# Moving a routing step behind two reductions in an attention + top-k mixture-of-experts kernel, and pinning its weight copies to slots

## The chip, the cores and the metric

The kernel runs on one core of one Trainium2 chip, in one launch. The metric is the device time of that launch in microseconds (us). A core has five engines with queues of their own, each of which works strictly in its order: PE (TensorE, matrix products and transposes), DVE (VectorE), ACT (ScalarE), POOL (GpSimd) and SP (SyncE, which here only issues transfers). Transfers run on 16 DMA engines, whoever issued them.

## The reference

Attention with normalised queries and keys over 8 batches, 12 heads, 448 positions, 64 dimensions, and then a gated mixture of 8 experts over the 3584 resulting rows of width 768:

```python
q_n, k_n = rmsnorm(q, g_q), rmsnorm(k, g_k)        # x / sqrt(mean(x*x) + 1e-6) * g
scores = matmul(q_n, k_n.T) / sqrt(64)
attn = softmax(scores)
x = matmul(attn, v).transpose(0, 2, 1, 3).reshape(N, 768)
logits = x @ w_gate                                 # 768 x 8
expert_idx = argmax(logits); gate_w = softmax(logits)[expert_idx]
for e in range(8):                                  # the 80 rows of largest gate_w of each expert
    out[tok] = gate_w[tok] * (relu(x[tok] @ w1[e]) @ w2[e])      # w1 768x1024, w2 1024x768
```

Rows that no expert keeps are zero in the output.

## The kernel before, in words

**Tiling.** A *group* `g` is four heads of one batch, so there are 24 groups (`NG`), three (`NQ`) to a batch `b`. A group has 7 *blocks* (`RD`) of 64 keys. For each of the 168 blocks, `score` (L351) lets PE multiply 64 keys by all 448 queries for the four heads into the PSUM tile `ps` (PSUM is the small memory that PE writes), and ACT takes the exponential into `at` (L362). `av` (L365) multiplies by the values `vt` into `po`, and `presum` (L387) adds the `at` tiles up on DVE into `sm`, the denominators-to-be, at L392 and L394.

**Preparing a group.** For q (`a` = 0) and k (`a` = 1): ACT squares the loaded tile `qk` into `sq` (`square`, L270). DVE reduces it to the sums of squares `ms` (`squares`, L278). `rstd` (L286) lets ACT take a logarithm and an exponential of `ms` into `rs` (L289, L290) and DVE refine `rs` with three small instructions (L291 to L293). `normalise` (L300) lets DVE multiply `qk` by `rs` into `qn` (L306). `transp` (L328) transposes `qn` on PE into a PSUM tile `tp`, which ACT copies out as `qkT` (L349 for k, L347 for q).

**Routing a batch.** After a batch's third group, `zl` (L396) lets PE compute 48 products to unnormalised logits and denominators. `gate1` and `gate1t` copy, add and transpose them. `gate1v` (L439) takes the reciprocals `rz` (L445, the *quotients*), multiplies (`lx`, L453) and sends `rz` off by SP (L460). `gate2` (L465) sums to the logits `lg` (L468) and finds the maximum and the equality mask `eq`. `gate2x` (L480) is ACT's exponential `lex` and the copy `eqb`. `gate2b` (L486) sums and inverts to the gate weight `gw`. `gate2i` and `gate2p` are POOL's share: it packs `gw` and row numbers into `info` (L504 to L521). `merge` (L524) then keeps a running list of the best 80 rows of each expert; its steps `row` (transposes `gw` on PE, copied by ACT at L543), `experts`, `own`, `counts`, `place`, `turn` are mixes of small PE, ACT and DVE work.

**What sets the order.** It is written out by hand. There are 84 *slots* (`NS`), each with two score blocks and the two `av` of the slot before. Four tables say what else a slot emits: `begins`, `pre` (behind the scores), `mid` (behind `presum`) and `end`, with `ahead` in front of `end`. Each engine receives its part in that order. `b0` is the slot in which a batch's last group starts (in the second table loop) or in which a group starts (in the first). With 10.5 slots to a batch, odd and even batches meet the groups' preparation differently.

**PSUM tiles.** `ps`, the k-side `tp`, `zl` and the scratch tiles of `merge` take turns in two buffers named `sc`. PE can't begin a `ps` before ACT has emptied the tile two turns back.

**The weights.** Experts 0 to 2 are loaded once into SBUF, converted to bf16 on the way (`fetch_held`, L669; POOL issues, behind a small DVE memset of the tile). The others are converted into a scratch in DRAM (`stage_w`, L201, two halves for each matrix, POOL issues, nothing in front of it) and fetched later by SP (`fetch_late`). The output is first filled with zeros by SP.

**The tail.** After the last slot come the last batch's routing and the eight experts in turn (L966 on).

Of the kernel before, what the change touches and what calls it, by code (L numbers as in the profile page):

```python
# [11 lines left out]
BF16 = mybir.dt.bfloat16  # L12
# [9 lines left out]
def kernel(  # L22
# [13 lines left out]
    nc = tc.nc  # L36
# [3 lines left out]
    E = moe_w_gate.shape[1]  # L40
# [13 lines left out]
    NQ = H // 4  # L54
# [9 lines left out]
    NW0 = 3  # L64
    wb_dram = nc.dram_tensor("wb_scratch", (E - NW0, 2, DM * F), BF16, kind="Internal").ap()

    cpool = ctx.enter_context(tc.tile_pool(name="const", bufs=1))
# [130 lines left out]
    def staged(e, i):  # L198
        return wb_dram[e - NW0, i].rearrange("(c p f) -> p c f", p=128, c=(DC, FC)[i])

    def stage_w(e, i, half):  # L201
        src = (moe_w1, moe_w2)[i][e].rearrange("(c p) f -> p c f", p=128)
        c = src.shape[1] // 2
        nc.gpsimd.dma_start(out=staged(e, i)[:, half * c:half * c + c],
                            in_=src[:, half * c:half * c + c])
# [27 lines left out]
    with av_stack:  # L233
# [117 lines left out]
        def score(r):  # L351
            g, x = divmod(r, RD)
            T0, T1 = st[g]["T0"], st[g]["T1"]
            ps = scps.tile([128, 2, 512], F32, tag="sc", name="ps")
            at = apool.tile([128, 2, S], F32, tag="at", name="at")
            for u in range(2):
                for hh in range(2):
                    d = slice(hh * D, (hh + 1) * D)
                    nc.tensor.matmul(ps[u * 64:u * 64 + 64, hh, :S],  # L359
                                     T1[d, u, x * 64:(x + 1) * 64], T0[d, u, :],  # L360
                                     start=True, stop=True)
            nc.scalar.activation(at[:], ps[:, :, :S], AF.Exp)  # L362
            st[g]["at%d" % x] = at

        def av(r):  # L365
            g, x = divmod(r, RD)
            vt, at = st[g]["v"], st[g]["at%d" % x]
            if x == 0:
                po = pops.tile([128, 2, 512], F32, tag="po", name="po")
                other = po if g < NG - 1 else tpps.tile([128, 2, 512], F32, tag="tp", name="po")  # L370
                st[g]["po"] = (po, other)
            po = st[g]["po"]
            for u in range(2):
                p = slice(u * 64, u * 64 + 64)
                for hh in range(2):
                    nc.tensor.matmul(po[u][hh * D:(hh + 1) * D, u, :S],  # L376
                                     vt[p, hh * NX + x, :], at[p, hh, :],
                                     start=(x == 0), stop=(x == RD - 1))
            if x == RD - 1:
                st[g]["us"] = upool.tile([128, 2, S], F32, tag="us", name="us")  # L380

                n = 2 if g < NG - 1 else 1
                nc.scalar.copy(st[g]["us"][:, :n], po[0][:, :n, :S])  # L383
                if n < 2:
                    nc.vector.tensor_copy(st[g]["us"][:, n:], po[1][:, n:, :S])

        def presum(r):  # L387
            g, x = divmod(r, RD)
            s = st[g]
            if x == 1:  # L390
                s["sm"] = smpool.tile([128, 2, S], F32, tag="psm", name="sm")
                nc.vector.tensor_add(s["sm"][:], s["at0"][:], s["at1"][:])  # L392
            elif x > 1:
                nc.vector.tensor_add(s["sm"][:], s["sm"][:], s["at%d" % x][:])  # L394
# [298 lines left out]
        begins, pre, mid, end = {}, {}, {}, {}  # L693

        def at_slot(where, s, f, *a):
            where.setdefault(s, []).append((f, a))

        ahead = {}

        def first(s, f, *a):  # L700
            ahead.setdefault(s, []).append((f, a))
# [15 lines left out]
        for g in range(NG):  # L717
            b0 = g * RD // 2
            at_slot(begins, max(b0 - 11, -10), load_qk, g)
            at_slot(begins, b0 - 4, load_v, g)  # L720
            if g:
                for a in range(2):
                    at_slot(mid, b0 - 7 + a if g > 1 else -1, square, g, a)
                    at_slot(end, b0 - 7 + a if g > 1 else -1, squares, g, a)
                at_slot(mid, b0 - 5 if g > 1 else 0, rstd, g)
                for a in range(2):
                    at_slot(mid, b0 - 5 + a if g > 1 else 0, normalise, g, a)
            if g:
                for a in (0, 1) if g == 1 else (1, 0):
                    at_slot(end, b0 - 2 + (a if g == 1 else 0), transp, g, a)  # L730
            if g < NG - 2:
                i = g % NQ
                x0 = ((NQ * (g // NQ) - 1) * RD // 2 + 10 + 3 * i) if g >= NQ else 6 + 3 * i
                at_slot(end, b0 + 6 if i == NQ - 1 else x0, xout, g)
        for b in range(B):
            b0 = (NQ * b + NQ - 1) * RD // 2
            if b == B - 1:
                at_slot(end, b0 + 3, zl, b, range(NQ - 1))
                at_slot(end, b0 + 4, xout, NG - 2)
                at_slot(end, b0 + 4, zl, b, range(NQ - 1, NQ))  # L740
                at_slot(end, b0 + 4, gate1, b)
                at_slot(end, b0 + 4, xout, NG - 1)
                at_slot(end, b0 + 5, gate1t, b)
                at_slot(mid, b0 + 6, gate1v, b)
                continue
            first(b0 + 5, zl, b, range(NQ))
            first(b0 + 5, gate1, b)
            at_slot(end, b0 + 6, gate1t, b)
            at_slot(mid, b0 + 7, gate1v, b)
            at_slot(mid, b0 + 7, gate2, b)  # L750
            at_slot(mid, b0 + 8, gate2i, b)
            at_slot(end, b0 + 8, gate2x, b)
            at_slot(pre, b0 + 9, gate2b, b)
            at_slot(pre, b0 + 9, gate2p, b)
            for t, fs in enumerate(merge(b)):


                if b == B - 2 and t > 3:
                    at_slot(end, b0 + 12 + t, fs[0])
                    continue  # L760
                s = 15 + b % 2 if b < B - 2 else 13
                (first if t else lambda *a: at_slot(end, *a))(
                    b0 + (10, 10, 12, s, 18 + b % 2, 20 + b % 2)[t], fs[0])
                for n, f in enumerate(fs[1:]):
                    at_slot(end, b0 + (10, 11, 12, s)[t], f)
        at_slot(begins, 0, load_wgs)
        at_slot(end, NS - 6, weights_early)
        at_slot(end, NS, weights_late)
# [7 lines left out]
                in_=zeros[:, :].unsqueeze(1).to_broadcast([128, DM // ZW, ZW])))  # L776
        for e in range(E):
            for i in range(2):
                s = 9 + 23 * (2 * e + i) // 5
                if e < NW0:  # L780
                    at_slot(mid, s, fetch_held, e, i)
                    continue
                for half in range(2):
                    at_slot(begins, s + 2 * half, stage_w, e, i, half)


        wps = scps.tile([128, 2, 512], F32, tag="sc", name="wps")
# [3 lines left out]
        for s in range(-10, NS + 6):  # L791
            for f, a in begins.pop(s, []):
                f(*a)
            S2 = [r for r in (2 * s, 2 * s + 1) if 0 <= r < NG * RD]
            A2 = [r for r in (2 * s - 2, 2 * s - 1) if 0 <= r < NG * RD]

            for r in A2:
                if r % RD == RD - 1 and r < A2[-1]:
                    av(r)
            for r in S2:  # L800
                score(r)
            for f, a in pre.pop(s, []):
                f(*a)
            for r in A2:
                presum(r)
            for f, a in mid.pop(s, []):
                f(*a)
            for r in A2:
                if r % RD < RD - 1 or r == A2[-1]:
                    av(r)  # L810
            for f, a in ahead.pop(s, []) + end.pop(s, []):
                f(*a)
        assert not ahead
        assert not begins and not pre and not mid and not end
    mpool = ctx.enter_context(tc.tile_pool(name="moe_sb", bufs=2))

# [11 lines left out]
    b = B - 1  # L828
# [27 lines left out]
    ahead = tpool.tile([128, NT, CAP], BF16, tag="ahead", name="ahead")  # L856
# [187 lines left out]
```

## Time and profile before

| | |
|---|---|
| time, median of 3 runs | 424.39 us (422.96 to 424.91) |
| the profiled execution | 423.0 us, its span 421.3 us |
| PE busy | 399.1 us, 95% |
| DVE busy | 357.5 us, 85% |
| ACT busy | 314.9 us, 75% |
| POOL busy | 73.5 us, 17% |
| granted PE clock | 0.998 of full speed |
| HBM read, written | 101.11 MB, 39.89 MB |

The span runs from the first instruction to the last; around it lie 1.7 us. Slots fill it from 15.6 us to about 356 us, the tail the rest. "Busy" counts an engine's instructions without its waits; an instruction of 128x896 elements takes about 1 us on DVE or ACT, and PE does a slot's 16 score rows in 1.5 us. In a row of the timeline, the bracket at the end is the time for which the engine stood idle before it, and what ended that.

### The profile page before, as it was taken

The numbers are of one execution on the slowest core, as the hardware profiler recorded it, in microseconds if no ns is written. First come the engines' busy times: TensorE is split into PE (matmuls) and PEld (weight loads), VectorE is DVE, ScalarE is ACT, GpSimd is POOL, SyncE is SP. The second block draws the span as 40 slices with busy tenths as digits, with TensorE's granted clock in tenths as the row PEclk, the third lists the DMA queues.
The fourth block names the chain that finished last, engine by engine and source line by source line (L and its number), as shares of the span: only waits on it lengthen the run. The fifth ranks groups of instructions, "written<-read, shape, count | busy, mean of one in ns | idle before, by whom it ended". The sixth has DMA issues, their size and how long they took to land.

```text
span 421.3 us, 12543 instructions
## 1 busy us (share of the span) xinstructions
PE 399.1 (95%) x5289; PEld 194.9 (46%) x5289; DVE 357.5 (85%) x641; ACT 314.9 (75%) x479; POOL 73.5 (17%) x118
## 2 busy tenths in 40 slices
PE   6799999999989999999899999999999999889993
PEld 6334444444444445444444444443444443448882
DVE  5699889998999999989999999989999779735550
ACT  5898979997889799979798799878997784202120
POOL 2000001301040205100420024001500050134321
PEclk9999999999999999999999999999999999999999
DMA  7355599999959999999799969999799298869981
GB/s 261 123 149 140 152 224 317 282 254 268 287 166 206 326 230 274 242 237 320 234 236 233 338 172 195 232 286 338 170 237 312 59 358 211 270 213 339 342 301 47
DMA packets 75983, 100.91 MB, mean 240 GB/s; under 512 B 8344, under 2 KB 65176, under 8 KB 75928
## 3 DMA queue, kind: packets, MB, share of 16 engines
q1 hardware_dynamic: 59856, 70.53, 52.2%
q0 software_dynamic: 15776, 29.13, 36.1%
q8 instruction: 41, 0.67, 0.6%
q10 hardware_dynamic: 296, 0.46, 0.4%
q14 instruction: 14, 0.11, 0.1%
HBM read 101.11 MB, written 39.89 MB: 335 GB/s over the span
## 4 chain that ended last, share of the span: by engine, by line
PE 69%; DMA 12%; DVE 10%; ACT 5%; issue 2%; SPq 0%; POOLq 0%; DVEq 0%; ACTq 0%
PE ps L359 26%; PE po L376 26%; DMA w_sb<-wb_scratch 5%; PE zl L411 4%; DMA qk<-in_k_dram 4%; PE tp L314 3%; PE xp L314 3%; DVE ms L278 2%; DVE sm L394 2%; DMA xr_scratch<-xb 2%; PE py L992 1%; DVE qn L306 1%; PE ph L973 1%; ACT qkT L349 1%; DMA xg<-xr_scratch,idxG 1%
## 5 line engine op out<-in xcount | busy, mean ns | idle before, releaser
L359 PE MATMUL ps<-qkT 64*64 64x448 f32 x1344 | 147.9, 548 | 7.6 <-ACT qkT L349 3.2
L362 ACT ACTIVATE at<-ps 128x896 f32<-128x896 f32 x168 | 146.4, 931 | 2.5 <-PE ps L359 1.6
L376 PE MATMUL po<-at,vt 64*64 64x448 f32 x1344 | 142.4, 537 | 0.1
L394 DVE TENSOR_TENSOR sm<-sm,at 128x896 f32<-128x896 f32 x120 | 132.0, 1100 | 2.9
L376 PEld LDWEIGHTS po<-at,vt 64*64 64x64 f32 x1344 | 50.0, 133 | 74.9 <-issue 64.3
L359 PEld LDWEIGHTS ps<-qkT 64*64 64x64 f32 x1344 | 43.1, 132 | 73.2 <-issue 23.5
L278 DVE TENSOR_REDUCE ms<-sq 128x14 f32<-128x896 f32 (+1 forms) x50 | 51.9, 1044 | 6.6 <-ACT sq L270 6.4
L306 DVE TENSOR_TENSOR qn<-qk,rs 128x896 f32<-128x896 f32 (+1 forms) x50 | 52.5, 1052 | 1.9
L270 ACT ACTIVATE sq<-qk 128x896 f32<-128x896 f32 (+1 forms) x50 | 46.3, 929 | 2.8 <-DMA qk<-in_q_dram 2.8
L518 POOL CAST pt<-gw 128x4 bf16<-128x4 f32 x8 | 6.9, 866 | 201.9 <-DVE gw L491 201.9
L977 ACT ACTIVATE h_sb<-ph 128x320 bf16<-128x320 f32 x16 | 7.0, 437 | 39.8 <-PE ph L973 39.8
L654 ACT COPY xb<-xp 128x1024 f32<-128x1024 f32 x24 | 24.3, 1011 | 9.7 <-PE xp L314 9.6
L314 PEld LDWEIGHTS tp<-ident,qn 64*128 64x128 f32 x672 | 23.4, 139 | 11.1 <-issue 5.3
L314 PE MATMUL tp<-ident,qn 64*128 64x64 f32 x672 | 26.9, 226 | 0.0
L383 ACT COPY us<-po 128x896 f32<-128x896 f32 (+1 forms) x24 | 21.4, 893 | 6.2 <-PE po L376 6.2
L392 DVE TENSOR_TENSOR sm<-at 128x896 f32<-128x896 f32 x24 | 25.9, 1081 | 0.0
L347 ACT ACTIVATE qkT<-tp,gqk 128x896 f32<-128x896 f32 x23 | 23.5, 1023 | 0.0
L349 ACT COPY qkT<-tp 128x896 f32<-128x896 f32 x24 | 21.9, 913 | 1.3 <-PE tp L314 1.2
L992 PE MATMUL py<-w_sb,h_sb 128*80 128x384 bf16 (+1 forms) x136 | 22.2, 317 | 0.6 <-DMA w_sb<-wb_scratch 0.6
L996 DVE TENSOR_SCALAR yo<-py,gwT 80x384 f32<-80x384 f32 (+1 forms) x16 | 9.5, 600 | 14.9 <-PE py L992 14.7
L411 PE MATMUL zl<-us,wgs 64*32 64x448 f32 x192 | 21.0, 540 | 0.0
L411 PE MATMUL zl<-sm,zsel 64*32 64x448 f32 x192 | 20.5, 540 | 0.0
(170 smaller groups left out, 412.0 us busy)
## 6 DMA issues: line engine op xcount, KB each, us to landing
wb_scratch<-in_moe_w_dram POOLq DMA_DIRECT2D x20, 768.0 KB, 14.9
w_sb<-wb_scratch SPq DMA_DIRECT2D x9, 1536.0 KB, 8.1
vt<-in_v_dram SPq DMA_DIRECT2D x24, 448.0 KB, 6.3
out_dram<-zeros SPq DMA_DIRECT2D x28, 384.0 KB, 8.2
qk<-in_q_dram SPq DMA_DIRECT2D x23, 448.0 KB, 5.0
qk<-in_k_dram SPq DMA_DIRECT2D x23, 448.0 KB, 6.6
xr_scratch<-xb SPq DMA_DIRECT2D x48, 192.0 KB, 10.2
w_sb<-in_moe_w_dram POOLq DMA_DIRECT2D x6, 1536.0 KB, 15.7
```

Of the source, the lines that this page charges most:

```text
L270: nc.scalar.activation(st[g]["sq%d" % a][:, lo:hi], st[g]["qk"][a][:, lo:hi], AF.Square)
L278: nc.vector.reduce_sum(out=st[g]["ms"][:, a, lo:hi], in_=st[g]["sq%d" % a][:, lo:hi], axis=AX.X)
L306: nc.vector.tensor_mul(qn[:].rearrange("p (x hh) d -> p hh x d", hh=2)[:, h0:h1], qk[:, lo:hi].rearrange("p (hh x) d -> p hh x d", x=NX), ...
L314: nc.tensor.transpose(o, w, one[p, p], tile_position=(p.start, 0))
L349: nc.scalar.copy(T[:], tp[:, :, :S])
L359: nc.tensor.matmul(ps[u * 64:u * 64 + 64, hh, :S], T1[d, u, x * 64:(x + 1) * 64], T0[d, u, :], start=True, stop=True)
L362: nc.scalar.activation(at[:], ps[:, :, :S], AF.Exp)
L376: nc.tensor.matmul(po[u][hh * D:(hh + 1) * D, u, :S], vt[p, hh * NX + x, :], at[p, hh, :], start=(x == 0), stop=(x == RD - 1))
L392: nc.vector.tensor_add(s["sm"][:], s["at0"][:], s["at1"][:])
L394: nc.vector.tensor_add(s["sm"][:], s["sm"][:], s["at%d" % x][:])
L411: nc.tensor.matmul(t[32 * c:32 * c + 32, r, :S], w, x, start=(i == 0), stop=(i == NQ - 1))
L992: nc.tensor.matmul(py[:, :c1 - c0], h_sb[:, fc, :], chunk(e, 1, fc)[:, c0:c1], start=(fc == 0), stop=(fc == FC - 1))
```

## The change

- `gate1v` moves from the middle of slot `b0 + 7` to its end, behind the sums of squares that stand there; `gate2` and `gate2i` move to the end of slot `b0 + 8`, `gate2x`, `gate2b` and `gate2p` to the end of slot `b0 + 9`.
- The q-side normalisation of a group that starts a batch (from the third batch on) goes to a new table `after`, emitted last in its slot, so that `gw` stands in front of it.
- The product `tied` of `merge` goes one slot later.
- The weights: `fetch_held` takes other slots, and each half of `stage_w` gets a slot of its own in `mid`, held there by a one-element DVE memset of `mark` and a POOL copy of that element in front of the DMA.

```diff
+    mark = cpool.tile([1, 4 * (E - NW0)], BF16, name="mark")
+
     def stage_w(e, i, half):
+        n = 4 * (e - NW0) + 2 * i + half
+        nc.vector.memset(mark[:, n:n + 1], 0.0)
+        nc.gpsimd.tensor_copy(mark[:, n:n + 1], mark[:, n:n + 1])
...
-        ahead = {}
+        ahead, after = {}, {}
...
                 for a in range(2):
-                    at_slot(mid, b0 - 5 + a if g > 1 else 0, normalise, g, a)
+                    s = b0 - 5 + a if g > 1 else 0
+                    at_slot(after if not a and g % NQ == 0 and g > NQ else mid, s, normalise, g, a)
...
-            at_slot(mid, b0 + 7, gate1v, b)
-            at_slot(mid, b0 + 7, gate2, b)
-            at_slot(mid, b0 + 8, gate2i, b)
-            at_slot(end, b0 + 8, gate2x, b)
-            at_slot(pre, b0 + 9, gate2b, b)
-            at_slot(pre, b0 + 9, gate2p, b)
+            at_slot(end, b0 + 7, gate1v, b)
+            at_slot(end, b0 + 8, gate2, b)
+            at_slot(end, b0 + 8, gate2i, b)
+            at_slot(end, b0 + 9, gate2x, b)
+            at_slot(end, b0 + 9, gate2b, b)
+            at_slot(end, b0 + 9, gate2p, b)
...
                 for n, f in enumerate(fs[1:]):
-                    at_slot(end, b0 + (10, 11, 12, s)[t], f)
+                    at_slot(end, b0 + (10, 11 + n, 12, s)[t], f)
...
-                s = 9 + 23 * (2 * e + i) // 5
+                n = 2 * e + i
                 if e < NW0:
-                    at_slot(mid, s, fetch_held, e, i)
+                    at_slot(mid, 4 + 9 * n // 2, fetch_held, e, i)
                     continue
                 for half in range(2):
-                    at_slot(begins, s + 2 * half, stage_w, e, i, half)
+                    at_slot(mid, 4 + 9 * (2 * n + half) // 4, stage_w, e, i, half)
...
-            for f, a in ahead.pop(s, []) + end.pop(s, []):
+            for f, a in ahead.pop(s, []) + end.pop(s, []) + after.pop(s, []):
                 f(*a)
```

PE's and SP's queues keep their order. DVE's queue at batch 1, from the end of slot 24 on, before (`rz` to `eq` are the routing's quotients and logits, `ms` the sums of squares of q and k):

```order
L445 RECIPROCAL rz<-zs 128x12x2 x2
L453 TENSOR_TENSOR lx<-zs,rz 128x12x8 x4
L468 TENSOR_REDUCE lg<-lx 128x32
L471 TENSOR_REDUCE lmax<-lg 128x4
L474 TENSOR_TENSOR lex<-lg,lmax 128x32
L476 TENSOR_TENSOR eq<-lg,lmax 128x32
L477 MEMSET eq 64x8
L278 TENSOR_REDUCE ms<-sq 128x14
L394 TENSOR_TENSOR sm<-sm,at 128x896
L278 TENSOR_REDUCE ms<-sq 128x14
L489 TENSOR_REDUCE lsum<-lex 128x4
L491 RECIPROCAL gw<-lsum 128x4
```

and in the changed kernel (lines shift by 5):

```order
L283 TENSOR_REDUCE ms<-sq 128x14
L450 RECIPROCAL rz<-zs 128x12x2 x2
L458 TENSOR_TENSOR lx<-zs,rz 128x12x8 x4
L399 TENSOR_TENSOR sm<-sm,at 128x896
L283 TENSOR_REDUCE ms<-sq 128x14
L473 TENSOR_REDUCE lg<-lx 128x32
L476 TENSOR_REDUCE lmax<-lg 128x4
L479 TENSOR_TENSOR lex<-lg,lmax 128x32
L481 TENSOR_TENSOR eq<-lg,lmax 128x32
L482 MEMSET eq 64x8
```

Both sums of squares now stand in front of the logits; `lsum` and `gw` follow eight rows later, behind two `sm` additions and the three small `nw`, `rs` instructions.

ACT's queue at the same place, before (`lex` and `eqb` are the routing's, `rs` belongs to the normalisation, `qkT` are the copies of the transposed k and q):

```order
L481 ACTIVATE lex<-lex 128x32
L483 CAST eqb<-eq 128x288
L362 ACTIVATE at<-ps 128x896 x2
L289 ACTIVATE rs<-ms,eps 128x28
L290 ACTIVATE rs<-rs 128x28
L349 COPY qkT<-tp 128x896
L347 ACTIVATE qkT<-tp,gqk 128x896
```

and in the changed kernel:

```order
L367 ACTIVATE at<-ps 128x896 x2
L294 ACTIVATE rs<-ms,eps 128x28
L295 ACTIVATE rs<-rs 128x28
L354 COPY qkT<-tp 128x896
L352 ACTIVATE qkT<-tp,gqk 128x896
L486 ACTIVATE lex<-lex 128x32
L488 CAST eqb<-eq 128x288
```

The routing's two instructions moved from in front of the exponentials to behind the copies.

## Rows read from the trace of the kernel before

**Rows 1.** Busy time by engine in stretches from one zl to the next.
```profile
core 0: us, PE busy (x) PEld busy (x) DVE busy (x) ACT busy (x) POOL busy (x), PEclk, DMA share, GB/s
98.10:144.50 46.40, 44.61 (x600) 19.73 (x599) 43.72 (x76) 39.25 (x59) 6.61 (x10) 1.00 0.95 245
144.50:185.54 41.04, 40.93 (x570) 18.40 (x568) 39.67 (x69) 37.12 (x57) 10.32 (x16) 1.00 1.09 253
...
272.97:319.40 46.43, 44.99 (x604) 19.65 (x603) 43.60 (x72) 39.49 (x60) 7.30 (x11) 1.00 1.03 257
```
**Rows 2.** Waits of PE: us in total, times, longest us.
```profile
PE ps L359 <- ACT qkT L349: 3.2, 3, 1.2
...
PE ps L359 <- ACT row L543: 1.3, 3, 0.4
```
**Rows 3.** Timeline of PE, slots 26 to 28: start, us, instructions, idle before.
```profile
116.00 1.08 PE L314 MATMUL tp<-ident,qn 64*128 64x64 f32 x28
117.02 0.98 PE L359 MATMUL ps<-qkT 64*64 64x448 f32 x8
119.24 0.98 PE L359 MATMUL ps<-qkT 64*64 64x448 f32 x8 [1.24 <-ACT qkT L349]
...
121.76 0.33 PE L314 MATMUL mp<-identb,eqb 64*72 64x64 bf16 x8
...
124.20 0.98 PE L359 MATMUL ps<-qkT 64*64 64x448 f32 x8 [0.44 <-ACT row L543]
```
**Rows 4.** Timeline of ACT, the same slots.
```profile
114.47 0.23 ACT L481 ACTIVATE lex<-lex 128x32 f32<-128x32 f32 x1 [0.96 <-DVE lex L474]
...
115.04 1.72 ACT L362 ACTIVATE at<-ps 128x896 f32<-128x896 f32 x2
117.81 0.32 ACT L289 ACTIVATE rs<-ms,eps 128x28 f32<-128x28 f32 x1 [1.06 <-DVE ms L278]
...
118.30 0.89 ACT L349 COPY qkT<-tp 128x896 f32<-128x896 f32 x1
...
119.98 1.72 ACT L362 ACTIVATE at<-ps 128x896 f32<-128x896 f32 x2
```
**Rows 5.** Timeline of DVE, slots 22 to 28.
```profile
101.70 0.63 DVE L424 TENSOR_TENSOR zsb<-zsb,zo 128x448 f32<-128x448 f32 x1 [1.54 <-ACT zo L423]
...
112.00 0.46 DVE L445 RECIPROCAL rz<-zs 128x24 f32<-128x24 f32 x2
...
113.14 0.85 DVE L468 TENSOR_REDUCE lg<-lx 128x32 f32<-128x384 f32 x1
...
114.70 1.09 DVE L278 TENSOR_REDUCE ms<-sq 128x14 f32<-128x896 f32 x1
...
116.70 1.08 DVE L278 TENSOR_REDUCE ms<-sq 128x14 f32<-128x896 f32 x1
117.69 0.18 DVE L489 TENSOR_REDUCE lsum<-lex 128x4 f32<-128x32 f32 x1
...
120.85 1.09 DVE L306 TENSOR_TENSOR qn<-qk,rs 128x896 f32<-128x896 f32 x1
121.86 2.47 DVE L394 TENSOR_TENSOR sm<-sm,at 128x896 f32<-128x896 f32 x2
...
125.29 0.06 DVE L671 MEMSET w_sb<- 128x1 uint32 x1
```
**Rows 6.** The page's group of the sm additions: busy, mean ns, idle before.
```profile
L394 DVE TENSOR_TENSOR sm<-sm,at 128x896 f32<-128x896 f32 x120 | 132.0, 1100 | 2.9
```
**Rows 7.** Timeline of POOL, two rows behind the routing of batches 1 and 4.
```profile
120.92 1.34 POOL L512 TENSOR_TENSOR info<-eq,pt 128x160 bf16<-128x160 f32 x1
...
253.75 3.03 POOL L204 DMA_DIRECT2D wb_scratch<-in_moe_w_dram  x4
```
**Rows 8.** Timeline of SP: the issue of one load of q.
```profile
266.85 0.42 SPq L242 DMA_DIRECT2D qk<-in_q_dram  x1
```
**Rows 9.** Timeline of ACT: the square that needs that load.
```profile
284.67 0.96 ACT L270 ACTIVATE sq<-qk 128x896 f32<-128x896 f32 x1 [0.98 <-DMA qk<-in_q_dram]
```

More of the change, by code (lines that the diff above doesn't have):

```diff
@@ L810 @@
                     av(r)
-            for f, a in ahead.pop(s, []) + end.pop(s, []):
+            for f, a in ahead.pop(s, []) + end.pop(s, []) + after.pop(s, []):
                 f(*a)
-        assert not ahead
+        assert not ahead and not after
         assert not begins and not pre and not mid and not end
```

## The prediction

> **What bounds the kernel now.** I first read the page's busy shares: PE works 95% of the span at full clock, so the kernel can gain only where PE stands still or where it does less, and the change takes nothing from PE. To find where PE stands still I cut the slots into stretches from one batch's `zl` to the next [rows 1]. An even batch's stretch is full: 40.93 us busy of 41.04. An odd batch's stretch has 1.79 us without PE (46.40 less 44.61), and the one that ends at 319.40 is just as long. Batches 1, 3 and 5 make three such stretches. The list of waits then names the cause [rows 2]: three waits of a score for ACT's copy of the transposed k, 3.2 us together, and three for ACT's copy of `row`, 1.3 us together. There is nothing else of size inside the slots. So the question is what holds ACT at these two points.
>
> PE's timeline shows the place [rows 3]: the first score tile of slot 27 starts at 117.02, the second should follow about 0.80 later and starts at 119.24, so 1.42 us are lost; the second tile of slot 28 comes at 124.20, and about 0.6 is lost there (its gap is 0.44 beside a modelled end). ACT's timeline gives the reason [rows 4]: the copy L349 that frees the `sc` buffer starts at 118.30, because in front of it in ACT's queue `rs` waited 1.06 us for DVE's second sum of squares. DVE's timeline ends the search [rows 5]: DVE has no pause there; the k-side `ms` starts at 116.70 because quotients and logits (112.00 to 114.70, 2.70 us) stand in front of both sums. That is the work which the change puts elsewhere.
>
> **The change part by part.** *The sums of squares.* I walk DVE's new queue with the old durations. At 112.00 the q-side `ms` runs (1.00 us from start to start, as 116.70 to 117.69). Then the quotients take 113.14 - 112.00 = 1.14, to 114.14. One `sm` addition takes about 1.0, to 115.14. The k-side `ms` then ends at 115.14 + 1.09 = 116.23 [rows 5]. Before, it ended at 117.78. So `rs` can start 1.55 us earlier, about 116.27 instead of 117.81. From the start of `rs` to that of L349 are 0.49, and from there to the exponentials 1.68 [rows 4]; so L349 starts at 116.76 (the k half of `tp` is written by about 116.6 [rows 3]). PE's second score came 0.94 behind the start of L349 (118.30, 119.24). By that it may start at 117.70, before PE is ready for it at 117.82: the first stall goes.
>
> *What is late next.* ACT's own work. `lex` and `eqb` used to run while ACT had nothing else, and now stand between L347 and the exponentials of slot 27: 115.04 - 114.47 = 0.57 [rows 4]. Those exponentials start at 116.76 + 1.68 + 0.57 = 119.01 instead of 119.98 and end at 120.73. The transposes of `eqb` need the buffer that the second exponential frees (before: 121.70, and they started at 121.76 [rows 3]), so PE waits for them until 120.79; from there to the second score of slot 28 were 2.44 us (124.20 - 121.76), filled by ACT's copies in a row. That gives 123.23 in place of 124.20: **0.97 us at a place, 2.9 us for three**. Half of the old stall stays, as a wait for ACT's exponentials and `row`.
>
> *The gate weight.* `gw` comes later: logits to 116.23 + 1.56 = 117.79, then two additions, three small instructions, `lsum` and `gw`, the same set that ran from 117.69 to 120.85 [rows 5], so 120.95. PE's `row` transposes come 0.66 behind the `eqb` ones, at 121.45. The cover is 0.5 us; if it is gone, each us of `gw` costs a us there. DVE's `lsum` waits for ACT's `lex`, done by 118.7, and meets no wait at 120.6. Behind it in DVE's queue stands the q-side normalisation, which begins at 120.95 against 120.85 before, and isn't wanted by PE for two slots. POOL's packing moves three us later; its `info` is used much later.
>
> *Even batches.* There ACT has no idle time in front of `rs`, and the two small ACT instructions only change places with the exponentials. I take 0.06 us a batch, a tenth of the 0.57 that they last, and 0.2 together; the bounds are 0 and 0.57 each.
>
> *DVE's room.* DVE is nearly full: in 46.40 us it pauses 1.54 once, waiting for `zl` [rows 5]. A gain above 1.5 us at a place would move the bound to DVE. 0.97 fits.
>
> *The marks.* Twenty memsets and twenty POOL copies. The nearest memset takes 0.06 us and its neighbours keep their pace [rows 5]. For the copies the trace has a bound: while POOL ran `info` (160 elements), DVE's pair of additions at 121.86 took 2.47 us, where two at the mean of 1.10 take 2.2: 0.27 lost [rows 5 to 7]. A copy of one element costs DVE between 0 and 0.27; I take 0.03, near the lower end, since it moves one element for 160. That is 0.6 us over the whole run, which lies in DVE's pauses. At 0.27 each the nine copies in an odd and an even stretch would cost DVE 2.4 us.
> The Trainium skill ("SBUF — State Buffer", Who interferes with whom) has VectorE instructions with two SBUF inputs and GpSimd instructions that read SBUF exclude each other, the later one blocked for the whole of the other. The `info` row agrees in kind: 0.27 us lost beside 1.34 of POOL. By that rule a copy can hold up an addition, and if each does so for as long as `info` did, the time is that of the third rival.
>
> *The copies' slots.* The halves now go out one in about 2.25 slots, where four went out within 3 us behind a routing [rows 7]. The total stays. One load of q issued at 266.85, after such a burst, was needed by a square that waited 0.98 until 284.67 [rows 8, 9]. It is why batch 5's stall was only 3.2 - 2 x 1.24 = 0.7 us: PE had lost the other 0.55 earlier. So with the stall gone, this late load could be what remains in batch 5; paced copies should take it away. I take 0 beyond the 0.97, with bounds of 0.5 either way.
>
> The tail isn't touched: same instructions, same fetches, and its time counts from the last slot.
>
> **The sum.** 2.9 - 0.2 = 2.7 us. Against the profiled execution, 421.3 of span and 1.7 around it, this is 420.3. The median of the runs shown is 424.39, 1.4 above the profiled one, and by it 421.7. I name 421.4, nearer the median.
>
> **Rivals.** *All of it comes back.* If the ACT chain has slack that I don't see, a place gains up to DVE's pause, 1.54, and batch 5 the 0.55 of the late load as well: 5 us, 419.4. For it: the stalls are 2.0 us at a place. Against: ACT's copies in front of 124.20 follow each other without a pause.
> *Nothing is left.* The slots run nearly full on PE, DVE and ACT together; `gw` may come after PE wants it, or the gained time turns up as a wait of ACT for later sums of squares, as DVE doesn't get faster. 424. Against: DVE pauses at each odd `zl`, so a lag doesn't carry on.
> *The copies block DVE.* The 2.4 us in an odd and an even stretch exceed DVE's one pause of 1.54 by 0.9, so such a pair would be 0.9 longer than now in place of 0.97 shorter: 2.7 in three, 427.1. It decides from 0.17 us a copy on, where the pause is gone. Against: the smallness of the copies.
> *Slower: loads come late.* If with a copy always under way loads of q and k land later than about 16.8 us behind their issue (17.8 less the 0.98 waited [rows 8, 9]), ACT waits at the squares. At 0.55 us of PE for each wait, eleven such waits of the 46 cost 6.0; less the 2.7 gained, 427.7. It decides from five waits on. For it: the DMA share is near 1 in these stretches [rows 1]. Against: the bursts, not the mean, made the one late load.
>
> **How the numbers follow.** Forecast 0.57, all back 0.11, nothing left 0.23, copies block 0.04, late loads 0.05. About 0.5%, 2.1 us, is what a measurement of this kernel can tell from no change. The forecast is past it by 0.6 to 0.9 us, and I give a sixth of its chance to the near side. Faster 0.59, same 0.32, slower 0.09. The forecast's own range is 419.8 to 422.8. Down to 418.4 it takes in the full recovery from a low base, up to 424.8 the cases that leave nothing; the two slower ones are left out.
>
> **What would show it.** In the changed profile's waits, the copy of the transposed k no longer holds a score (below 0.3 us in all); a wait for ACT's exponentials or `row` stays, about 1 us a place. The odd stretches are near 45.4 us, the even ones 41.0. `rs` starts within 0.1 of the end of `ms` and about 18.2 us behind the start of `zl`. Squares don't wait for loads. It is wrong if the odd stretches stay at 46.4, if PE waits for `gw`, if DVE's pause at `zl` is gone, or if squares wait for q or k.

## The result, and the profile after

The changed kernel takes 419.64 us (median of 6 runs, 419.13 to 420.85); the kernel before took 424.34 beside it (6 runs, 422.83 to 424.91). The ratio is 0.991 with a 95% interval of 0.9886 to 0.9934: faster by 0.7% to 1.1%. The prediction said 421.4 with a range of 418.4 to 424.8, and faster as the likeliest; its sum against the profiled execution said 420.3, and the profiled execution of the changed kernel took 420.0 (span 418.3).

These are the stretches from one `zl` to the next, with the columns of [rows 1]: the odd batch 1 and the even batch 2.

```profile
98.91:144.13 45.22, 44.44 (x600) 19.84 (x598) 42.93 (x75) 39.15 (x59) 7.26 (x11) 1.00 0.99 256
144.13:185.16 41.03, 40.91 (x568) 18.39 (x567) 39.78 (x74) 37.11 (x57) 8.52 (x16) 1.00 1.03 251
```

An odd stretch went from 46.40 to 45.22, an even one stayed at 41.03; those of batches 3 and 5 take 45.23. PE's busy time in the odd one is nearly the same (44.61, now 44.44); its time without work fell from 1.79 to 0.78. The three odd stretches give 3.5 us. The rest of the span's 3.0 is small and of both signs: the first score starts 0.72 later (13.28 instead of 12.56, in the loading of the first tiles, which the change leaves alone), the first even stretch is 0.08 longer, and the tail behind the last `zl` is 0.3 shorter.

The waits of PE in the changed kernel, as in [rows 2] (lines stand 5 later):

```profile
PE ps L364 <- ACT row L548: 1.3, 3, 0.4
...
PE mp L319 <- ACT at L367: 0.7, 3, 0.2
```

The wait for ACT's copy of the transposed k, 3.2 us in three before, is gone. The wait for `row` stayed at 1.3 in three, and a new one of 0.7 in three came up, for the exponentials. PE's timeline at the place of [rows 3]:

```profile
116.78 1.09 PE L319 MATMUL tp<-ident,qn 64*128 64x64 f32 x28
117.79 1.74 PE L364 MATMUL ps<-qkT 64*64 64x448 f32 x16
...
121.40 0.33 PE L319 MATMUL mp<-identb,eqb 64*72 64x64 bf16 x8 [0.22 <-ACT at L367]
...
122.06 0.43 PE L319 MATMUL mp<-ident,gw 64*128 64x64 f32 x8
122.42 0.98 PE L364 MATMUL ps<-qkT 64*64 64x448 f32 x8
123.84 0.98 PE L364 MATMUL ps<-qkT 64*64 64x448 f32 x8 [0.44 <-ACT row L548]
```

Both score tiles of slot 27 now run as one group of 16 rows; before, the second half waited 1.24. The second score of slot 28 comes 24.93 behind its `zl` (123.84 less 98.91), where it came 26.10 behind. ACT's timeline there, as in [rows 4]:

```profile
114.60 1.73 ACT L367 ACTIVATE at<-ps 128x896 f32<-128x896 f32 x2 [0.29 <-PE ps L364]
116.93 0.32 ACT L294 ACTIVATE rs<-ms,eps 128x28 f32<-128x28 f32 x1 [0.60 <-DVE ms L283]
...
117.47 0.91 ACT L354 COPY qkT<-tp 128x896 f32<-128x896 f32 x1
118.28 1.01 ACT L352 ACTIVATE qkT<-tp,gqk 128x896 f32<-128x896 f32 x1
119.18 0.23 ACT L486 ACTIVATE lex<-lex 128x32 f32<-128x32 f32 x1
119.30 0.43 ACT L488 CAST eqb<-eq 128x288 bf16<-128x288 f32 x1
119.62 1.73 ACT L367 ACTIVATE at<-ps 128x896 f32<-128x896 f32 x2
...
123.20 0.59 ACT L548 COPY row<-mp 128x512 f32<-128x512 f32 x1
123.68 0.94 ACT L367 ACTIVATE at<-ps 128x896 f32<-128x896 f32 x1
```

`rs` still waits for DVE, for 0.60 where it was 1.06, and from there to `row` ACT has one pause of 0.27. So the residual wait belongs to ACT's own sequence. DVE's timeline, as in [rows 5]:

```profile
102.50 0.63 DVE L429 TENSOR_TENSOR zsb<-zsb,zo 128x448 f32<-128x448 f32 x1 [1.27 <-ACT zo L428]
...
113.81 0.46 DVE L450 RECIPROCAL rz<-zs 128x24 f32<-128x24 f32 x2
...
114.82 1.08 DVE L399 TENSOR_TENSOR sm<-sm,at 128x896 f32<-128x896 f32 x1
115.82 1.08 DVE L283 TENSOR_REDUCE ms<-sq 128x14 f32<-128x896 f32 x1
116.81 0.87 DVE L473 TENSOR_REDUCE lg<-lx 128x32 f32<-128x384 f32 x1
...
121.29 0.18 DVE L496 RECIPROCAL gw<-lsum 128x4 f32<-128x4 f32 x1
...
122.38 2.21 DVE L399 TENSOR_TENSOR sm<-sm,at 128x896 f32<-128x896 f32 x2
```

The k-side `ms` ends at 116.90, 17.99 behind `zl` (19.68 before), and `rs` follows within 0.03. The pair of additions that took 2.47 against POOL's `info` now takes 2.21. The page's groups of the additions, as in [rows 6], and of the new copies on POOL:

```profile
L399 DVE TENSOR_TENSOR sm<-sm,at 128x896 f32<-128x896 f32 x120 | 130.5, 1087 | 2.9
...
L206 POOL COPY mark<-mark 1x1 bf16<-1x1 bf16 x20 | 7.5, 376 | 138.4 <-DVE mark L205 138.4
```

An addition takes 1087 ns on average, 13 less than before. Nearly all of that comes from `info`: before, six of the 120 additions took 1.35 us, one in each of six batches, each against an `info` of 1.34 to 1.35 us; now none takes more than 1.09, and `info` takes 0.46 (once 0.66), since it starts at another moment. POOL's timeline, as in [rows 7], shows the first of the weights' halves going out behind its copy (the next follow at 149.16, 156.67 and 164.90). The load of q that was issued at 266.85 and took 17.8 us before [rows 8, 9] now goes out at 263.94 and takes 7.8. ACT's row for its square, the last one below, has no bracket: ACT did not wait for it.

```profile
141.87 0.18 POOL L206 COPY mark<-mark 1x1 bf16<-1x1 bf16 x1 [15.40 <-DVE mark L205]
141.99 0.81 POOL L209 DMA_DIRECT2D wb_scratch<-in_moe_w_dram  x1
```
```profile
282.00 0.97 ACT L275 ACTIVATE sq<-qk 128x896 f32<-128x896 f32 x1
```

### The profile page after: what moved, and what is told of

Its sections match the earlier page's. It is cut to its first block, busy times and chain, and to the rows that moved or that the text cites. A ratio compares the mean times of both kernels' runs of the same rounds, so it can differ in the third digit from the quotient of the medians.

```text
span 418.3 us, 12587 instructions
## 1 busy us (share of the span) xinstructions
PE 398.7 (95%) x5289; PEld 195.6 (47%) x5289; DVE 355.3 (85%) x661; ACT 314.3 (75%) x479; POOL 80.6 (19%) x138
## 4 chain that ended last, share of the span: by engine, by line
PE 81%; DMA 7%; ACT 5%; DVE 3%; issue 2%; POOLq 0%; ACTq 0%
PE ps L364 32%; PE po L381 29%; DMA w_sb<-wb_scratch 5%; PE zl L416 5%; PE tp L319 4%; PE xp L319 3%; ACT at L367 1%; PE py L998 1%; PE ph L979 1%; DMA qk<-in_q_dram 1%; ACT zsb L426 1%; DMA xg<-xr_scratch,idxG 1%; PE mp L594 1%; ACT zo L428 1%; ACT xb L659 1%
## 5 line engine op out<-in xcount | busy, mean ns | idle before, releaser
L399 DVE TENSOR_TENSOR sm<-sm,at 128x896 f32<-128x896 f32 x120 | 130.5, 1087 | 2.9
L206 POOL COPY mark<-mark 1x1 bf16<-1x1 bf16 x20 | 7.5, 376 | 138.4 <-DVE mark L205 138.4
(172 smaller groups left out, 420.3 us busy)
```

## The experiments

Theory A is the prediction's: the whole gain comes from the k-side sum of squares ending earlier, what is left is ACT's own sequence up to `row`, and the weights' copies with their marks move almost nothing. The other theories that an expectation names hold what it says of them there.

The stretches tell more than the times. The runs of the changed kernel scatter by 1.7 and 2.1 us, those of the kernel before by 2.1 to 5.3. In the profiled executions such differences lie at the start and in the tail (the last section), while an undisturbed odd or even stretch of a kernel repeats within 0.03. "Slots" is the time from the first `zl` to the last, in the profiled execution; medians are of the runs of a kernel, with the kernel before on the same chip beside it.

| kernel | median us (range; runs) | ratio to before | odd stretch | even | slots |
|---|---|---|---|---|---|
| before | 422.36 (421.79 to 426.0; 15); 423.13 (421.82 to 427.1; 11) | 1 | 46.40 | 41.03 | 295.0 |
| changed | 419.24 (418.41 to 420.55; 6) | 0.9898 [0.9852, 0.9943] | 45.21 | 41.03 | 291.5 |
| gate only | 419.45 (418.69 to 420.22; 4) | 0.9898 [0.985, 0.9946] | 45.23 | 41.08, 41.60 | 292.2 |
| copies only | 422.34 (421.96 to 423.94; 10) | 0.9991 [0.9966, 1.0016] | 46.39 | 41.03 | 295.0 |
| logits early | 424.43 (1) | | 46.83 | 41.03 | 296.3 |
| row first | 419.24 (418.24 to 420.03; 6) | 0.9897 [0.9858, 0.9936] | 44.67 | 41.38 | 290.9 |
| row first, odd batches | 418.48 (417.44 to 419.2; 6) | 0.9865 [0.9821, 0.9909] | 44.66 | 41.17 | 290.2 |
| gate weight late | 420.51 (1) | | 45.31 | 41.03 | 292.2 |
| eight copies | 418.74 (1) | | 45.22 | 41.03 | 291.6 |
| no marks | 430.53 (1) | | 45.24 | 46.84, 46.74 | 303.2 |

The first value of before goes with gate only, copies only, logits early and row first; the second with the others. No marks ran on that second chip too, later.

### The routing's order alone

The changed kernel with the weights' copies in their old slots and without marks:

```diff
...
-        nc.vector.memset(mark[:, n:n + 1], 0.0)
-        nc.gpsimd.tensor_copy(mark[:, n:n + 1], mark[:, n:n + 1])
...
+                s = 9 + 23 * (2 * e + i) // 5
...
-                    at_slot(mid, 4 + 9 * n // 2, fetch_held, e, i)
+                    at_slot(mid, s, fetch_held, e, i)
...
-                    at_slot(mid, 4 + 9 * (2 * n + half) // 4, stage_w, e, i, half)
+                    at_slot(begins, s + 2 * half, stage_w, e, i, half)
```

> The changed routing order with the weight copies as before (old slots, no marks). Theory A (the sums of squares in front of the logits make all of the gain): odd stretches between the starts of zl are 45.2 us as in the changed kernel (46.4 before), even ones 41.0, the wait of a score for the copy of the transposed k is gone, and the time is 3 to 4 us below before, level with the changed kernel within 0.6 us. Rival B (the copies' slots carry a part, since the medians differ by 4.7 us and three stretches only explain 3.5): the odd stretches are as in the changed kernel, but the time is 1 us or more above it; in batch 5 the late load of q shows again, and that stretch is 45.5 to 46.0.

The three odd stretches are 45.22, 45.23 and 45.23, as in the changed kernel. What the copies' slots add lies in one even stretch; its window, and the row of ACT and PE in it:

```profile
230.69:272.30 41.61, 41.18 (x569) 18.40 (x567) 40.13 (x69) 37.23 (x57) 8.52 (x12) 1.00 0.92 240
```
```profile
241.88 0.95 ACT L270 ACTIVATE sq<-qk 128x896 f32<-128x896 f32 x1 [0.45 <-DMA qk<-in_q_dram]
```
```profile
243.68 1.73 PE L376 MATMUL po<-at,vt 64*64 64x448 f32 x16 [0.33 <-ACT us L383]
```

A square waits for its load of q, the copy of `us` queues behind it on ACT, and PE waits for that: 0.57 us of the stretch. Neither theory had it there: A expected even stretches of 41.0, B a late load in batch 5. So the routing's order is worth 2.9 us of the slots (295.0 to 292.2), the copies 0.6 on top.

### The copies alone

The kernel before with the new slots and marks: the same lines the other way round.

> The routing order of before with the new slots and marks of the weight copies. Theory A: odd stretches 46.4 us, the three waits of a score for the copy of the transposed k as before, 3 to 4 us in all since no late load eats a part of the third; the time is that of before within 0.8 us. Rival B: the time is 1 us or more below before. By the rival in which the POOL copies hold up VectorE, it is above before by 1 us or more.

Its waits of PE, the row of the transposed k:

```profile
PE ps L364 <- ACT qkT L354: 3.7, 3, 1.2
```

Nothing is gained: 422.34 beside 422.36. In [rows 2] this wait was 3.2; here the third is as long as the others, since PE no longer loses 0.5 to the late load first. The late load was hidden behind the stall, as the prediction had it, and its removal counts only once the stall is gone.

### The logits back in front of the k-side sum

```diff
-            at_slot(end, b0 + 8, gate2, b)
+            at_slot(end, b0 + 7, gate2, b)
```

> The changed kernel with the logits (gate2, gate2i) back in the slot of the quotients: behind the q-side sum of squares, still in front of the k-side one. Theory A (it is the k-side sum, the later one, that ACT's rs waits for): the k-side sum ends 1.56 us later, so rs starts about 1.5 us later, the copy of the transposed k holds the score again by about 1.1 us, and odd stretches are about 46.2 us. Rival C (the gain comes from the q-side sum or from the routing being spread over slots): odd stretches stay at 45.2.

Only `gate2` moves back; `gate2i`, which the expectation names too, gives DVE nothing to do before the last batch. The row of the transposed k in PE's waits, the window of batch 1, and ACT's rows at the place:

```profile
PE ps L364 <- ACT qkT L354: 3.8, 3, 1.3
```
```profile
98.37:145.19 46.82, 44.68 (x601) 19.75 (x599) 44.50 (x76) 39.59 (x61) 7.28 (x11) 1.00 0.98 253
```
```profile
118.06 0.32 ACT L294 ACTIVATE rs<-ms,eps 128x28 f32<-128x28 f32 x1 [2.28 <-DVE ms L283]
...
120.23 0.23 ACT L486 ACTIVATE lex<-lex 128x32 f32<-128x32 f32 x1
120.35 0.43 ACT L488 CAST eqb<-eq 128x288 bf16<-128x288 f32 x1
120.67 1.73 ACT L367 ACTIVATE at<-ps 128x896 f32<-128x896 f32 x2
```

The wait for the transposed k is back, 3.8 us in three. `rs` starts 19.69 behind `zl`, 1.67 later than in the changed kernel, and the odd stretch is 1.60 longer. It is also 0.43 longer than before the change, although `rs` stands where it stood then (19.71): `lex` and `eqb` now come behind the copies, not in ACT's pause in front of `rs`, so the exponentials start 22.30 behind `zl` instead of 21.88. This splits the change at a place into two parts: **1.60 gained by the earlier sum, 0.43 given back by ACT's two small instructions, 1.17 net**. The expectation had 46.2 and missed that second part; the rival's 45.2, no effect, is refuted. The moves of `gate1v` and of `tied` were not tried alone; these two parts leave nothing at the place for them to explain.

### `row` ahead of `xb`

ACT's copy `xb` of the transposed outputs (1.01 us) stands in front of `row`. This kernel emits the step `row` directly behind `experts`:

```diff
-            for t, fs in enumerate(merge(b)):
+            for t, fs in sorted(enumerate(merge(b)), key=lambda p: (1, 0).index(p[0]) if p[0] < 2 else p[0]):
...
-                (first if t else lambda *a: at_slot(end, *a))(
+                first(
```

> The changed kernel with the step row of merge emitted directly behind experts, in front of xout, so that ACT copies row before xb. Theory A (what is left at an odd place, 0.66 us, is ACT's own sequence of copies, with row last): the wait of 0.44 us for row goes, the 0.22 us for the exponentials stays, odd stretches are 44.8 us, the time is 1.3 us below the changed kernel. Rival D (VectorE's rate already sets the odd stretches): they stay at 45.2 and its pause at zl doesn't shrink, or row is held up by gw, which is ready only about 0.1 us before PE wants it, and stretches are 45.2 or longer.

The odd stretches fall to 44.67, a little below the expected 44.8: the wait for `row` was ACT's sequence. The even ones rise by 0.35, since there PE now waits for ACT's `listT` (0.8 in 3), and the last stretch by 0.3. So the slots are only 0.6 us shorter than the changed kernel's, and the median, on another chip, is the same 419.24; the expected 1.3 did not come. The same edit was then made for the odd batches alone (`b % 2` in both conditions):

> The changed kernel with row directly behind experts in the odd batches alone. In the run with row first everywhere the odd stretches fell by 0.56 us and the even ones, which had no stall, grew by 0.35. Theory A: odd stretches 44.67 us, even ones back at 41.03, the slots 1.7 us shorter than in the changed kernel, the time 1.2 to 1.8 us below it. Rival D (VectorE sets the rate, so what the odd stretches win the even ones lose): the even stretches stay near 41.38 and the time is within 0.7 us of the changed kernel.

Windows of batches 1 and 2:

```profile
97.87:142.53 44.66, 44.33 (x601) 19.86 (x599) 42.38 (x74) 38.91 (x59) 7.47 (x11) 1.00 0.98 255
142.53:183.70 41.17, 41.04 (x568) 18.29 (x566) 39.92 (x73) 37.10 (x57) 8.48 (x15) 1.00 1.04 253
```

PE's time without work in an odd stretch is 0.33, from 0.78. The even stretches come back to 41.17, not to the expected 41.03; what the other 0.14 is was not followed. The slots are 1.4 us shorter than the changed kernel's, where 1.7 was expected. The odd stretches keep their gain, so DVE's rate does not set them; the time, 0.8 below the changed kernel's, lies between the two theories and decides nothing. By the medians this is the fastest version, 418.48 beside 419.24 and 423.13, but its interval against before overlaps that of the changed kernel; the stretches, not the times, carry the difference. The changed kernel itself ran beside it:

> The changed kernel once more, on the same chip as the others of this call. Stretches of 45.2 and 41.0 us; a ratio to before of 0.989 to 0.993. If the slots alone make the gain, the median is 3.3 to 3.9 us below before; the 4.7 us of the first measurement would then be partly scatter of the two medians.

On this chip it is 3.9 below before, between the lowest runs 3.4 (421.82 and 418.41), with stretches as in the first profile.

### The gate weight behind the normalisation

```diff
-                    at_slot(after if not a and g % NQ == 0 and g > NQ else mid, s, normalise, g, a)
+                    at_slot(mid, s, normalise, g, a)
```

> The changed kernel with the q-side normalisation back in front of lsum and gw (the table after unused). VectorE finishes gw about 1.0 us later, 0.4 us behind the point at which PE wants it for row. Theory A (ACT's copies set the end of the place, and row's copy begins 1.1 us behind PE's transposes): PE waits about 0.4 us for gw in odd batches, but the odd stretches stay at 45.2 to 45.3. Rival E (the gate weight is the next bound, as the prediction had it: each us of gw beyond its cover costs one): odd stretches are 45.6 us.

PE's two rows at slot 27 and 28:

```profile
123.61 0.45 PE L319 MATMUL mp<-ident,gw 64*128 64x64 f32 x8 [0.53 <-DVE gw L496]
123.98 1.73 PE L364 MATMUL ps<-qkT 64*64 64x448 f32 x16
```

PE waits 0.53 for `gw`, in all three odd batches, and the stretch grows by 0.09 only. The second score then follows the first without a gap, as the two form one group of 16: the wait for `row` had been in the same place, and the two lie on top of each other. In the first even stretch, 0.39 longer, PE waits 0.34 for the step `own`. The table `after` is worth 0.7 us in all.

### Eight copies to a mark

```diff
-        nc.gpsimd.tensor_copy(mark[:, n:n + 1], mark[:, n:n + 1])
+        for _ in range(8):
+            nc.gpsimd.tensor_copy(mark[:, n:n + 1], mark[:, n:n + 1])
```

> The changed kernel with eight POOL copies of the mark in place of one, 160 in all, 72 in an odd and an even stretch together. Theory A (a POOL copy waits for the VectorE addition under way and holds up the next one by 0 to 0.03 us): VectorE's additions stay at a mean of 1.09 us, stretches at 45.2 and 41.0, and each copy on POOL takes up to 1 us when additions run. Rival F (each copy holds up VectorE by 0.2 us or more): 7 us or more of additions are lost in each pair of stretches, VectorE's pause at zl is gone and the stretches grow by several us.

The page's groups of the additions and of the copies:

```profile
L400 DVE TENSOR_TENSOR sm<-sm,at 128x896 f32<-128x896 f32 x120 | 130.5, 1088 | 2.9
...
L207 POOL COPY mark<-mark 1x1 bf16<-1x1 bf16 x160 | 65.8, 412 | 88.0 <-DVE mark L205 79.5
```

With 160 copies the additions take 1088 ns instead of 1087, and the stretches are the same. A copy costs DVE nothing that can be seen; the prediction's 0.03 was too much and the rival that needs 0.17 is refuted. POOL does the waiting: a copy takes 0.18 us alone, 0.41 on average, and up to 1.67 where it waited out two DVE operations in a row. The Trainium skill ("SBUF — State Buffer", Who interferes with whom) has the instruction that was issued first hold the other off for its whole length, in either direction. In this trace the copies show the one direction, POOL waiting for additions. `info` shows both in the kernel before: it started 0.07 us behind `qn` (120.92 and 120.85 [rows 5, 7]), took 1.34 us where it takes 0.46 alone, and the addition behind `qn` then lost 0.26.

### The new slots without the marks

```diff
-    mark = cpool.tile([1, 4 * (E - NW0)], BF16, name="mark")
...
-        nc.vector.memset(mark[:, n:n + 1], 0.0)
-        nc.gpsimd.tensor_copy(mark[:, n:n + 1], mark[:, n:n + 1])
```

> The changed kernel without the marks: each half copy stands at its new place in POOL's queue, with nothing that holds it there. Theory A (the marks pace the transfers, but pacing is worth little, since loads were late once at most): the halves go out in bursts behind POOL's packing, four within 3 us as before; odd stretches 45.2 us, even ones 41.0, of which one or two may be up to 0.6 us longer by a late load of q or k. Rival B (pacing carries a part of the gain): several stretches are longer by 0.5 us or more, 2 us in all.

Theory A missed here by 10 us. The windows of batches 2 and 4, and POOL's issues in front of the second:

```profile
143.66:190.50 46.84, 44.22 (x568) 19.60 (x567) 40.52 (x69) 37.52 (x57) 7.71 (x11) 0.93 0.95 241
...
235.73:282.46 46.73, 42.65 (x568) 18.66 (x566) 40.53 (x69) 37.32 (x57) 7.74 (x11) 0.96 0.93 236
```
```profile
217.93 3.00 POOL L204 DMA_DIRECT2D wb_scratch<-in_moe_w_dram  x4
221.42 0.77 POOL L204 DMA_DIRECT2D wb_scratch<-in_moe_w_dram  x1
```

The odd stretches keep their 45.24; each of two even ones is 5.7 to 5.8 longer. Nothing holds the halves at their slots: POOL's packing waits for `gw` (35.63 us, up to 213.12), the halves collect behind it in its queue, and five go out within 4.3 us. The load of q that SP issues at 231.69 lands at 250.52, 18.8 us later. SP's issue, ACT and PE:

```profile
231.69 1.77 SPq L242 DMA_DIRECT2D qk<-in_q_dram  x1
```
```profile
250.55 0.95 ACT L270 ACTIVATE sq<-qk 128x896 f32<-128x896 f32 x1 [4.09 <-DMA qk<-in_q_dram]
```
```profile
252.34 3.23 PE L376 MATMUL po<-at,vt 64*64 64x448 f32 x16 [3.97 <-ACT us L383]
```

PE stands for 3.97 us, and the group behind takes 3.23 instead of 1.68: the granted clock was at 0.50 (1.2 GHz) behind the gap. So the marks, not the slots, do the work of that half of the change, and the rival of late loads was real as a mechanism. Against the old slots they are worth only the 0.6 of the first experiment.

The number of halves does not make this difference. In front of the other long stretch only four went out, and the kernel before sends five together too: a fifth follows the four of [rows 7]. POOL's issues here, then that one of the kernel before:

```profile
125.94 2.32 POOL L204 DMA_DIRECT2D wb_scratch<-in_moe_w_dram  x3
...
128.67 0.78 POOL L204 DMA_DIRECT2D wb_scratch<-in_moe_w_dram  x1
```
```profile
257.25 0.82 POOL L204 DMA_DIRECT2D wb_scratch<-in_moe_w_dram  x1
```

In every kernel without marks a load of q issued 8 to 14 us behind the start of such a burst takes 17 to 19 us, where its landing was recorded: 17.8 before the change, 16.7 and 17.4 in the first experiment, 18.8 twice and 16.7 here. What differs is how far behind its issue the square wants it, and how much later it lands. Before the change it was wanted 16.8 us behind its issue and came 0.98 late; in the first experiment 16.3 and 0.45; here 16.2 and 2.64, and 14.8 and 4.09. Only the last two left gaps of PE after which the clock fell. Why the loads were slower or wanted sooner here was not separated; the order of the routing lets POOL's packing end some 3 us later, in the first experiment as well.

## Why the prediction was right, and where it was off

**The stall.** "The first stall goes": shown. The wait for the transposed k is gone, `rs` starts 18.02 behind `zl` (predicted 18.17) and within 0.03 of the end of `ms`, and the third experiment brings the stall back when it puts the logits back.

**What is late next.** Right in kind and place: ACT's sequence, shown by moving one step of it (44.67). The size was 0.97 at a place and came out at 1.17. The offsets from `zl` say where the 0.20 is: the quotients take 1.01 (113.81 to 114.82) and not 1.14 (1.13 in the third experiment, where the logits, which read them, stand behind them again), `lex` and `eqb` hold ACT for 0.44 (119.18 to 119.62) and not 0.57, less 0.06 elsewhere on the way to the exponentials. Durations read in one neighbourhood were carried into another.

**The gate weight.** That PE wouldn't wait for it was right; "each us of `gw` costs a us there" was wrong. The late gate weight made PE wait 0.53 and cost 0.09, as the wait took the place of the 0.44 for `row`. This step wasn't needed for the sum.

**Even batches.** Predicted 0.06 each; they changed by 0.00, the first by 0.08.

**DVE's room.** The pause at `zl` stays: 1.27, 1.72 and 1.78 in the three odd stretches. They were 1.54, 1.70 and 1.70 before. By the prediction's walk, 1.54 less 0.97 would have been left. DVE's busy time in the stretch of batch 1 fell from 43.72 [rows 1] to 42.93, but 0.59 of that is a sum of squares that the end of the second window cuts: DVE has that work then still in front of it. The one real saving that was found is the 0.26 of the pair that stood against `info`.

**The marks.** Predicted at 0.6 us of DVE beside other work; nothing is visible even with eight times as many.

**The copies' slots.** Predicted 0 ± 0.5, with batch 5's late load as what would remain: it is 0.6, just past that bound, and in the first experiment the late load stood in batch 4's stretch. The four halves within 3 us that the prediction read in [rows 7] were five within 4.3. That without marks the same slots cost 11.6 us was no step of the prediction. Its rival of late loads put the limit at 16.8 us from issue to need, and the two loads that came late there took 18.8; but it priced such a wait at 0.55 us of PE, and these two cost 5.7 to 5.8 each.

**The sum.** The predicted sum in the slots, 2.7, became 3.45. That the prediction's profiled sum, 420.3, agrees with the profiled 420.0 is in part luck: the slots gave 0.75 more, and the first score, which started 0.72 later, took that back; the remaining 0.3 is the tail. The mis-sized step was the last one, where 1.1 us were added towards a median of three runs. That median stood on two of three runs that were long, 424.39 and 424.91, beside 422.96; the changed kernel's six lie in two groups as well, 419.13 to 419.27 and 420.02 to 420.85. Between the lowest runs the gain is 3.7, between the medians 4.7, on the second chip 3.4 and 3.9, in the spans 3.0. In the profiled executions everything beside these 3.45 lies outside the slots; the long runs of the kernel before were not profiled, so where their time goes is not shown.

## What to carry to other kernels

Where an engine waits, look at what stands in front of the awaited instruction in its producer's queue, and ask whether that is wanted later than the thing behind it: here 1.6 us of routing stood in front of a sum that PE needed, and nobody needed the routing yet. Count in the same breath where the moved step's followers come to stand, as they gave back 0.43 of the 1.60; two waits at one place overlap and must not be added. A transfer without a wait of its own goes out whenever its queue is free, not in the slot in which the code has it, and a burst of four or five 768 KB copies was enough to make a 448 KB load take 17 to 19 us. Whether that cost nothing, half a microsecond or nearly six depended here on how soon the load was wanted and how late it came.

## What the runs showed of the hardware that was not expected

**The clock behind a pause of PE.** At the start PE waits for the product of the two gains `g_q` and `g_k` (L95), for 1.2 to 2.3 us. In six of the eleven profiles the granted clock then fell to 0.50: for 6.8 us behind pauses of 2.29 in gate only and gate weight late, which cost 1.3 to 1.4 us by the first `zl`, and for 3.4 us behind 1.71 to 2.13 in copies only, logits early, row first and no marks, which cost 0.2 to 0.6. It stayed at 1.00 behind 1.76 in the kernel before, behind 2.09 and 1.45 in the changed kernel's two profiles, and behind 1.19 and 1.36 in row first for odd batches and eight copies. So the length of the pause alone does not decide. One window of the first experiment (the clock is the third number from the end):

```profile
14.00:16.00 2.00, 2.00 (x16) 0.39 (x12) 1.71 (x2) 1.63 (x3) 0.00 (x0) 0.50 0.00 2
```

Row first for odd batches had the clock at 0.50 for 3.4 us in the tail, and its tail is 1.5 us longer than that of the changed kernel's repeat. Of the changed kernel's first six runs the two with a mean granted clock of 0.987 and 0.988 took 420.69 and 420.85, the four with 0.993 to 0.996 took 419.13 to 420.02. A good part of the scatter goes with the clock; the moment at which the first tiles land is another part, 13.28 and 12.25 for the first score in the changed kernel's two profiles.

**A late load costs more than its wait.** Without marks, gaps of 2.51 and 3.97 us each lengthened their stretch by 5.7 to 5.8: behind the shorter gap the clock was at 0.50 for about 7 us, behind the longer one for about 3.4. The gap and half of that time add up to 5.9 and 5.7. So the loss did not follow the length of the gap alone.

**With short copies it is POOL that waits.** A one-element copy lasts from 0.18 to 0.97 us on POOL in the changed kernel, since it waits out the addition under way; 160 of them cost DVE's additions at most 1 ns each on average.
